# The opening of a fused retention and low-rank mixer kernel: its hand-written order written anew

## The chip, the cores and the metric

The kernel runs on one core of a Trainium2 chip. A core has a matrix engine (PE, with its weight loads listed apart as PEld), a vector engine (DVE), a scalar engine (ACT), a third elementwise engine (POOL) and a queue engine (SP) that here does nothing but issue transfers. Each engine takes its own instructions strictly in the order in which the program lists them; engines wait for one another through semaphores. The metric is device time in microseconds (us) of one execution.

## The reference

There are two parts. The first is a retention recurrence over a sequence of 768 steps, for 4 batches and 8 heads of width 64:

```
state = gamma[h] * state + outer(k[t], v[t])
y[t]  = scale * q[t] @ state
```

Its heads are laid side by side to x, 768 x 512 for each batch, and the second part is a mixer on x:

```
h   = xt @ U @ V                  # xt: x with rows and columns exchanged; rank 32
u   = x + h (turned back)
out = u + relu(u @ w_ch1) @ w_ch2 # 512 -> 2048 -> 512
```

## The kernel before

The recurrence is computed in 6 chunks of 128 steps. With decay factors put onto q and k beforehand, a chunk c needs: q and k scaled (`qd`, `kd`), turned by PE so that the head width lies on partitions (`turn_q`, `turn_k`) and copied out of PSUM (`evict_q`, `evict_k`); the scores of the chunk with itself (`scores`), masked by DVE (`keep`); v cast to bf16 (`cast_v`); the running sum of k times v (`sums`), copied to a bf16 state (`state`); and the output as the product of q with the state of the chunks before (`inter`) plus masked scores times v (`intra`), copied to x (`evict_x`). The state makes this a chain: `inter(c)` needs `state(c-1)`, and `sums(c)` may not write the running sum before `state(c-1)` has read it.

Then the mixer: `low` multiplies x by U, `evict_P` copies the result, `turn_x` and `high` build u with channels on partitions in PSUM, `evict_u` copies it, and the first large product (`mlp1`, with w_ch1) and the second (with w_ch2, by a scheme with fewer block products) follow. While the MLP of batch b runs, the recurrence of batch b+1 is woven into it at numbered slots.

Only batch 0 has nothing to be woven into. Its recurrence, from the start to the first `mlp1` matmul, is the opening, or ramp. Its order is written out by hand: one list of calls (lines 811 to 839 of the kernel before), each with its chunk or half and, where an engine can be chosen, the engine: G for POOL, V for DVE, A for ACT. The list sets the order on every engine at once. It also holds `run_idle(n, bank)`: n matmuls of zeros, 128 x 512, whose result nobody reads; another nine of them stand ahead of the list.

The inputs of batch 0 are asked for by SP ahead of the list in a fixed order: q0, kA, q1, k2, k3, vA, q2, k4, v2, k5, v3, v4, v5. (q0, q1, q2 hold two chunks each; kA and vA hold chunks 0 and 1. For the first two chunks of q, and likewise for the other pairs, even and odd steps are apart, so `turn_q(0, h)` needs both `qd(0, 0)` and `qd(0, 1)`.) Nothing in the list touches that queue. The slices of w_ch1 are asked for from POOL's queue (`load_w1`, line 161), those of w_ch2 too (line 167).

A helper records most operations, so many have one line number: PE work is L116 apart from the transposes L334 (k) and L346 (q); copies are L310 on ACT and L312 on DVE or POOL; L327 is `qd`, L322 `kd`, L368 `keep`. In the names, bk is a PSUM bank, st the state, a the masked scores, vb the cast v, qk the scaled q and k, q0T and kT the turned ones.

Of the kernel before, what the change touches and what calls it, by code (L numbers as in the profile page):

```python
# [47 lines left out]
def kernel(  # L48
# [17 lines left out]
    DH = moe_w_ch1.shape[1]  # L66
# [238 lines left out]
    G, V, A = nc.gpsimd, nc.vector, nc.scalar  # L305
# [503 lines left out]
        copy_by(eng, uTs[0][:, c, ts(hf, HS)], r0["u", hf, c])  # L809

    for f, *args in (
        (qd, 0, 0, V), (qd, 0, 1, G), (run_idle, 9, 5), (turn_q, 0, 1), (turn_q, 0, 0), (kd, 1, V),
        (evict_q, 0, 0, A), (run_idle, 4, 5), (turn_k, 1), (evict_k, 1, A), (kd, 0, G),
        (turn_k, 0), (evict_q, 0, 1, V), (run_idle, 1, 5), (scores, 1), (qd, 1, 1, V),
        (qd, 1, 0, G), (run_idle, 1, 2), (turn_q, 1, 0), (evict_k, 0, A), (scores, 0), (kd, 2, G),
        (keep, 1, 0), (kd, 3, G), (keep, 1, 1), (evict_q, 1, 0, A), (turn_q, 1, 1),
        (evict_q, 1, 1, A), (keep, 0, 1), (keep, 0, 0), (qd, 2, 1, G), (spread_V, 0),
        (spread_V, 1), (evict_V, 1, A), (turn_k, 2), (evict_k, 2, V), (run_idle, 2, 1),
        (turn_k, 3), (evict_k, 3, V), (evict_V, 0, A), (kd, 4, G), (scores, 2), (cast_v, 1, V),
        (kd, 5, G), (cast_v, 0, A), (run_idle, 2, 1), (sums, 0), (keep, 2, 0), (state, 0, A),  # L820
        (intra, 0), (keep, 2, 1), (scores, 3), (evict_x, 0, A), (sums, 1), (inter, 1), (intra, 1),
        (qd, 2, 0, V), (turn_q, 2, 1), (keep, 3, 0), (load_w1, 0, 256), (load_w1, DH // 2, 256),
        (turn_k, 4), (turn_q, 2, 0), (keep, 3, 1), (evict_x, 1, V), (evict_k, 4, V), (state, 1, A),
        (inter, 2), (evict_q, 2, 1, A), (cast_v, 2, V), (run_idle, 1, 0), (sums, 2),
        (evict_q, 2, 0, A), (scores, 4), (intra, 2), (state, 2, A), (inter, 3), (evict_x, 2, A),
        (turn_k, 5), (keep, 4, 1), (evict_k, 5, A), (turn_x, 0, 0), (cast_v, 3, V), (sums, 3),
        (keep, 4, 0), (intra, 3), (scores, 5), (turn_x, 0, 2), (state, 3, V), (cast_v, 4, A),
        (keep, 5, 1), (evict_x, 3, A), (sums, 4), (state, 4, A), (keep, 5, 0), (inter, 4),
        (intra, 4), (low, (0, 1, 2, 3)), (inter, 5, 1), (cast_v, 5, G, 1), (cast_v, 5, G, 0),
        (intra, 5, 1), (evict_x, 5, V, 1), (evict_x, 4, A), (inter, 5, 0), (intra, 5, 0),  # L830
        (turn_x, 0, 3), (turn_x, 0, 1), (low, (4,)), (evict_x, 5, A, 0), (low, (5,)),
        (evict_P, 0, A), (turn_x, 1, 1), (turn_x, 1, 2), (turn_x, 1, 0), (evict_P, 1, A),
        (high, 0, 0), (high, 0, 1), (evict_u, 0, 0, V), (evict_u, 0, 1, V), (high, 1, 0),
        (evict_u, 1, 0, A), (high, 0, 2), (turn_x, 1, 3), (high, 1, 2), (high, 0, 3),
        (evict_u, 0, 2, V), (evict_u, 0, 3, V), (high, 1, 1), (evict_u, 1, 1, V), (high, 1, 3),
        (evict_u, 1, 3, A), (evict_u, 1, 2, V), (load_w1, 256, 768),
        (load_w1, DH // 2 + 256, 256),
    ):
        f(*args)

# [124 lines left out]
```

## Time and profile before

| what | value |
|---|---|
| runs of the kernel before | 221.0, 221.14, 221.19 us (median 221.14) |
| the profiled execution | 222.94 us |
| its span, first to last instruction | 221.2 us |
| PE busy in the span | 213.1 us (96%) |
| mean granted TensorE clock | 0.992 |
| first `mlp1` matmul | 29.84 us from the span's start |
| idle matmuls | 29 in all, 20 of them in the list |

The times in the profile are us from the span's start. A row of the timeline gives start, duration, engine, line, operation, output <- inputs, shape and count, and in brackets how long the engine had been idle and who ended that. Rows that merge several instructions start with the first and end with the last. A matmul's end in these rows is some 0.16 us after the next one may start, so the next matmul's start and not the end says how long PE was taken, while a reader of the result waits for the end. The view by stretches gives for each the busy time of the engines and the granted clock (1.00 is full speed). The chain of waits goes back from the last instruction to what released it.

### The profile page before, as it was taken

How to read it: one execution, taken by the hardware profiler on the slowest of the kernel's cores; microseconds unless marked ns; L12 is line 12 of the kernel's file. 1: busy time of each engine (PE TensorE's matmuls, PEld its weight loads, DVE VectorE, ACT ScalarE, POOL GpSimd, SP SyncE). 2: the span in 40 equal slices, each digit the busy share in tenths (PEclk: the TensorE clock that was granted, in tenths of full speed). 3: DMA queues.
4: the chain of work that ended last, by engine and by line, in shares of the span. 5: the costliest groups of instructions: out<-in, count | busy, mean ns of one | idle time of the engine just before them, and what ended most of it. 6: DMA issues, size and time to landing. Idle time of an engine off the chain costs nothing.

```text
span 221.2 us, 5022 instructions
## 1 busy us (share of the span) xinstructions
PE 213.1 (96%) x1999; PEld 155.0 (70%) x1999; DVE 147.0 (66%) x295; ACT 119.7 (54%) x248; POOL 81.8 (37%) x91
## 2 busy tenths in 40 slices
PE   7898999999999999999999999998999999999993
PEld 2446665668888765667887876666887866668883
DVE  8577784798887873579974720889885601556662
ACT  3346847775148466778444737778434557771000
POOL 6656820003996401904233279550424430000000
PEclk9969999999999999999999999999999999999999
DMA  6999999999999968999999389998020570000222
GB/s 170 237 268 189 142 204 214 212 216 221 196 223 183 224 160 165 187 210 308 149 217 235 75 159 237 226 232 126 3 95 3 125 181 30 0 0 0 98 95 96
DMA packets 98583, 34.89 MB, mean 158 GB/s; under 512 B 86752, under 2 KB 94848, under 8 KB 98560
## 3 DMA queue, kind: packets, MB, share of 16 engines
q1 hardware_dynamic: 94112, 30.02, 67.9%
q0 software_dynamic: 4304, 4.29, 12.0%
q8 instruction: 15, 0.25, 0.5%
q10 hardware_dynamic: 144, 0.26, 0.3%
q14 instruction: 8, 0.07, 0.1%
HBM read 27.46 MB, written 6.29 MB: 153 GB/s over the span
## 4 chain that ended last, share of the span: by engine, by line
PE 89%; DMA 4%; ACT 2%; DVE 2%; POOL 1%; issue 1%; SPq 0%; ACTq 0%
PE bk L116 87%; DMA in<-in_q_dram 4%; PE bk L440 1%; ACT st L310 1%; POOL qk L327 1%; ACT P_sb L121 1%; PE bk L334 1%; DVE vb L312 1%; SPq L176 0%; DVE gs L621 0%; PE bk L346 0%; DVE state L508 0%; ACT x L480 0%; DVE x L312 0%; DVE kT L312 0%
## 5 line engine op out<-in xcount | busy, mean ns | idle before, releaser
L116 PE MATMUL bk<-uT,w1b 128*128 128x384 bf16 x512 | 85.7, 326 | 0.0
L116 PEld LDWEIGHTS <-w1b 128*128 128x128 bf16 x512 | 53.8, 106 | 29.6 <-issue 0.2
L121 ACT ACTIVATE gT<-bk 128x384 bf16<-128x384 f32 x125 | 61.1, 490 | 23.6 <-PE bk L116 23.4
L697 DVE TENSOR_TENSOR res<-bk,res 128x256 f32<-128x256 f32 (+2 forms) x66 | 30.3, 461 | 20.7 <-PE bk L116 19.6
L116 PEld LDWEIGHTS <-gT 128*128 128x128 bf16 x384 | 36.1, 98 | 7.6 <-issue 1.9
L116 PE MATMUL bk<-w2b,gT 128*128 128x256 bf16 x288 | 37.6, 273 | 0.0
L116 PEld LDWEIGHTS <-gs 128*128 128x128 bf16 x296 | 27.8, 98 | 4.5 <-DVE gs L621 0.9
L268 POOL TENSOR_TENSOR qk<-k_n,Gk 128x512 bf16<-128x512 f32 x18 | 19.9, 1105 | 25.0 <-DMA k_n<-in_k_dram 23.7
L621 DVE TENSOR_TENSOR gs<-gT 128x768 bf16<-128x768 bf16 (+1 forms) x20 | 10.5, 526 | 27.7 <-ACT gT L121 27.7
L116 PE MATMUL bk<-w2s,gs 128*128 128x256 bf16 x192 | 25.9, 273 | 0.6 <-DVE gs L621 0.6
L463 DVE TENSOR_TENSOR a<-bk,mask 128x512 bf16<-128x512 f32 x36 | 22.9, 681 | 1.6 <-PE bk L116 1.3
L562 DVE TENSOR_TENSOR res<-bk,x 128x512 f32<-128x512 f32 x24 | 15.9, 686 | 9.3 <-PE bk L116 9.2
L697 POOL TENSOR_TENSOR res<-s,res 128x512 f32<-128x512 f32 (+2 forms) x13 | 13.7, 1060 | 21.6 <-DVE res L697 16.2
L480 ACT ACTIVATE x<-bk 128x512 bf16<-128x512 f32 x18 | 10.7, 596 | 19.2 <-PE bk L116 16.9
L273 POOL TENSOR_TENSOR qk<-q_n,Gq 128x512 bf16<-128x512 f32 x18 | 19.7, 1097 | 0.3
L697 POOL TENSOR_TENSOR res<-c,res 128x256 f32<-128x256 f32 x12 | 8.7, 725 | 18.1 <-ACT c L692 18.0
L116 PE MATMUL bk<-w2s,gT 128*128 128x256 bf16 x96 | 13.4, 273 | 0.0
L279 ACT ACTIVATE vb<-v_n 128x512 bf16<-128x512 f32 x18 | 10.9, 624 | 4.1 <-DMA v_n<-in_v_dram 4.0
L116 PE MATMUL bk<-w2b,gs 128*128 128x256 bf16 (+1 forms) x104 | 13.1, 264 | 0.0
L621 DVE TENSOR_TENSOR gs<-gs,gT 128x768 bf16<-128x768 bf16 (+1 forms) x20 | 11.8, 591 | 0.7
L621 DVE TENSOR_TENSOR gT<-gT 128x768 bf16<-128x768 bf16 (+1 forms) x20 | 12.0, 598 | 0.0
L116 PE MATMUL bk<-idle 128*128 128x512 bf16 x29 | 10.5, 505 | 1.2 <-DVE idle L190 1.2
(99 smaller groups left out, 221.0 us busy)
## 6 DMA issues: line engine op xcount, KB each, us to landing
k_n<-in_k_dram SPq DMA_DIRECT2D x22, 256.0 KB, 5.1
v_n<-in_v_dram SPq DMA_DIRECT2D x22, 256.0 KB, 5.1
out_dram<-res SPq DMA_DIRECT2D x22, 256.0 KB, 2.8
q_n<-in_q_dram SPq DMA_DIRECT2D x18, 256.0 KB, 5.1
w2b<-in_moe_w_ch_dram POOLq DMA_DIRECT2D x4, 512.0 KB, 15.0
in<-in_q_dram SPq DMA_DIRECT2D x3, 512.0 KB, 6.3
w1b<-in_moe_w_ch_dram POOLq DMA_DIRECT2D x3, 256.0 KB, 5.3
w1b<-in_moe_w_ch_dram POOLq DMA_DIRECT2D x1, 768.0 KB, 7.9
```

The source lines that it names most:

```text
L116: nc.tensor.matmul(o, l, r, **kw)
L121: nc.scalar.activation(o, i, AF.Relu if relu else AF.Copy)
L268: eng.tensor_tensor(kd, k_n, Gk[:, c].unsqueeze(2).to_broadcast([P, H, D]), op=ALU.mult)
L273: eng.tensor_tensor(qd, rc[b, c]["q_n"], Gq[:, c].unsqueeze(2).to_broadcast([P, H, D]), op=ALU.mult)
L279: nc.scalar.activation(vb, rc[b, c]["v_n"], AF.Copy)
L310: nc.scalar.activation(o, i, AF.Copy)
L312: eng.tensor_copy(out=o, in_=i)
L463: nc.vector.tensor_tensor(r["a"][:, e], r["s"][e].rearrange("p (n t) -> p n t", n=NP), mask4, op=ALU.mult)
L480: nc.scalar.activation(x_of(b, c), o, AF.Copy)
L562: nc.vector.tensor_tensor(res_of(b, j), h, xs[b, j], op=ALU.add)
L621: nc.vector.tensor_tensor(o, x, y, op=op)
L697: eng.tensor_tensor(x, y, x, op=ALU.add)
```

## The change

The list of the opening is written anew. The same operations stand in it, for the same chunks and halves, in another order, and some go to another engine:

- from POOL to DVE: `kd(0)`, `kd(3)`; `qd(1, 0)` goes from POOL to DVE and `qd(1, 1)` from DVE to POOL; `qd(0, 0)` and `qd(0, 1)` trade places likewise.
- from DVE to ACT: `evict_k(2)`, `evict_k(3)`, `evict_x(1)`, `evict_q(0, 1)`, `evict_u(0, 0)`, `evict_u(0, 2)`, `evict_u(1, 2)`; from ACT to DVE: `evict_q(0, 0)`, `evict_k(1)`, `evict_x(4)`, half 1 of `evict_P`. `cast_v(0)` and `cast_v(1)` trade ACT and DVE.
- the idle matmuls in the list are 7, 9, 3, 1, 6, 2, 2 (30), before 9, 4, 1, 1, 2, 2, 1 (20). Eleven stand behind the turning of q1 (`turn_q(1, 0)`), before five.
- `load_w1` for the first two slices of 256 columns stands 16 and 13 entries earlier in the list, the other `load_w1` entries six.

Two lines of the list, which has 135 entries:

```diff
-        (qd, 0, 0, V), (qd, 0, 1, G), (run_idle, 9, 5), (turn_q, 0, 1), (turn_q, 0, 0), (kd, 1, V),
+        (qd, 0, 1, V), (qd, 0, 0, G), (run_idle, 7, 5), (turn_q, 0, 0), (qd, 1, 1, G), (kd, 1, V),
...
+        (evict_q, 1, 0, A), (evict_q, 1, 1, A), (turn_k, 2), (keep, 0, 1), (run_idle, 6, 1),
```

ACT's queue, from the eviction of q's second pair (`evict_q(1, 0)`, q0T) to that of x of chunk 0. Before:

```order
L310 ACTIVATE q0T_189<-bk1_12_264 128x2x2x128
L310 ACTIVATE q0T_189<-bk0_15_295 128x2x2x128
L310 ACTIVATE Vb_95<-bk7_17_307 128x384
L310 ACTIVATE Vb_95<-bk6_16_305 128x384
L310 ACTIVATE vb_0_0_344<-in0_97 128x512
L310 ACTIVATE st0_185<-bk7_24_349 64x4x64 x2
L310 ACTIVATE x_0_0_390<-bk6_25_361 128x512
```

and after:

```order
L310 ACTIVATE q0T_189<-bk1_11_269 128x2x2x128
L310 ACTIVATE q0T_189<-bk0_14_296 128x2x2x128
L310 ACTIVATE Vb_95<-bk6_16_304 128x384
L310 ACTIVATE kT_0_2_325<-bk3_18_311 128x512
L310 ACTIVATE Vb_95<-bk7_15_302 128x384
L310 ACTIVATE vb_0_1_346<-in0_97 128x512
L310 ACTIVATE st0_185<-bk7_22_350 64x4x64 x2
L310 ACTIVATE kT_0_3_390<-bk2_24_362 128x512
L310 ACTIVATE x_0_0_392<-bk6_25_370 128x512
```

The evictions of k of chunk 2 and of chunk 3 (kT_0_2, kT_0_3) have come in from DVE, the one ahead of the cast of v, the other between the state and x.

POOL's queue, from the scaling of q's second pair to the third slice of w_ch1. Before:

```order
L327 TENSOR_TENSOR qk_2_260<-in_97,Gq_168 128x512
L322 TENSOR_TENSOR qk_2_260<-k_n_2_101,Gk 128x512
L322 TENSOR_TENSOR qk_3_258<-k_n_3_103,Gk 128x512
L327 TENSOR_TENSOR qk_5_303<-in_97,Gq_168 128x512
L322 TENSOR_TENSOR qk_4_328<-k_n_4_107,Gk 128x512
L322 TENSOR_TENSOR qk_5_303<-k_n_5_111,Gk 128x512
L161 DMA w1b_428<-in_moe_w_ch_dram 128x4x256
L161 DMA w1b_430<-in_moe_w_ch_dram 128x4x256
L312 CAST vb_5_569<-v_n_5_117 128x256 x2
L161 DMA w1b_633<-in_moe_w_ch_dram 128x4x768
```

and after:

```order
L327 TENSOR_TENSOR qk_3_209<-in_97,Gq_168 128x512
L322 TENSOR_TENSOR qk_2_267<-k_n_2_101,Gk 128x512
L327 TENSOR_TENSOR qk_5_327<-in_97,Gq_168 128x512
L322 TENSOR_TENSOR qk_4_330<-k_n_4_107,Gk 128x512
L322 TENSOR_TENSOR qk_5_327<-k_n_5_111,Gk 128x512
L161 DMA w1b_348<-in_moe_w_ch_dram 128x4x256
L161 DMA w1b_367<-in_moe_w_ch_dram 128x4x256
L312 CAST vb_5_519<-v_n_5_117 128x256 x2
L161 DMA w1b_637<-in_moe_w_ch_dram 128x4x768
```

The scaling of k of chunk 3 has gone; the transfers of w_ch1 stand behind the same two instructions, the scalings of k4 and k5, as before.

DVE's queue, from the scaling of q's third pair to the cast of v of chunk 3. Before:

```order
L327 TENSOR_TENSOR qk_0_4_328<-in0_97,Gq0_168 128x512
L368 TENSOR_TENSOR a_0_3_381<-bk4_26_379,mask_174 128x512
L368 TENSOR_TENSOR a_0_3_381<-bk5_27_380,mask_174 128x512
L312 CAST x_0_1_443<-bk6_28_400 128x512
L312 COPY kT_0_4_445<-bk3_30_432 128x512
L312 CAST vb_0_2_455<-v_n_0_2_109 128x512
L368 TENSOR_TENSOR a_0_4_466<-bk5_35_465,mask_174 128x512
L312 CAST vb_0_3_504<-v_n_0_3_113 128x512
```

and after:

```order
L327 TENSOR_TENSOR qk_0_4_330<-in0_97,Gq0_168 128x512
L368 TENSOR_TENSOR a_0_3_404<-bk4_26_402,mask_174 128x512
L312 CAST vb_0_2_420<-v_n_0_2_109 128x512
L312 COPY kT_0_4_466<-bk3_30_445 128x512
L368 TENSOR_TENSOR a_0_3_404<-bk5_27_403,mask_174 128x512
L368 TENSOR_TENSOR a_0_4_476<-bk5_35_475,mask_174 128x512
L312 CAST vb_0_3_503<-v_n_0_3_113 128x512
```

x of chunk 1 has gone to ACT, and the cast of v of chunk 2 stands three instructions further forward, ahead of the eviction of k4 and of one of chunk 3's masks.

More of the change, by code (lines that the diff above doesn't have):

```diff
@@ L811 @@
     for f, *args in (
-        (qd, 0, 0, V), (qd, 0, 1, G), (run_idle, 9, 5), (turn_q, 0, 1), (turn_q, 0, 0), (kd, 1, V),
[L813 to L835, printed above, removed]
@@ L836 @@
-        (evict_u, 1, 3, A), (evict_u, 1, 2, V), (load_w1, 256, 768),
-        (load_w1, DH // 2 + 256, 256),
+        (qd, 0, 1, V), (qd, 0, 0, G), (run_idle, 7, 5), (turn_q, 0, 0), (qd, 1, 1, G), (kd, 1, V),
+        (kd, 0, V), (run_idle, 9, 5), (turn_q, 0, 1), (evict_q, 0, 0, V), (turn_k, 0), (turn_k, 1),
+        (evict_k, 1, V), (evict_q, 0, 1, A), (run_idle, 3, 5), (scores, 1), (evict_k, 0, A),
+        (qd, 1, 0, V), (turn_q, 1, 0), (scores, 0), (keep, 1, 1), (kd, 2, G), (keep, 1, 0),
+        (turn_q, 1, 1), (keep, 0, 0), (spread_V, 1), (spread_V, 0), (run_idle, 1, 2), (kd, 3, V),
@@ new lines @@
+        (evict_q, 1, 0, A), (evict_q, 1, 1, A), (turn_k, 2), (keep, 0, 1), (run_idle, 6, 1),
+        (evict_V, 0, A), (evict_k, 2, A), (qd, 2, 1, G), (evict_V, 1, A), (kd, 4, G), (kd, 5, G),
+        (scores, 2), (cast_v, 0, V), (cast_v, 1, A), (load_w1, 0, 256), (sums, 0), (run_idle, 2, 1),
+        (turn_k, 3), (load_w1, DH // 2, 256), (keep, 2, 1), (intra, 0), (keep, 2, 0), (state, 0, A),
+        (evict_k, 3, A), (evict_x, 0, A), (sums, 1), (scores, 3), (qd, 2, 0, V), (keep, 3, 0),
+        (inter, 1), (cast_v, 2, V), (state, 1, A), (intra, 1), (turn_q, 2, 1), (turn_k, 4),
@@ new lines @@
+        (evict_x, 1, A), (turn_q, 2, 0), (evict_q, 2, 1, A), (inter, 2), (run_idle, 2, 0),
+        (evict_k, 4, V), (keep, 3, 1), (sums, 2), (evict_q, 2, 0, A), (scores, 4), (intra, 2),
+        (keep, 4, 1), (state, 2, A), (turn_k, 5), (evict_x, 2, A), (cast_v, 3, V), (inter, 3),
+        (sums, 3), (evict_k, 5, A), (cast_v, 4, A), (keep, 4, 0), (cast_v, 5, G, 1), (intra, 3),
+        (turn_x, 0, 1), (state, 3, V), (scores, 5), (turn_x, 0, 0), (turn_x, 0, 2), (sums, 4),
+        (evict_x, 3, A), (keep, 5, 0), (state, 4, A), (inter, 4), (intra, 4), (keep, 5, 1),
@@ new lines @@
+        (low, (0, 1, 2, 3)), (inter, 5, 0), (inter, 5, 1), (cast_v, 5, G, 0), (evict_x, 4, V),
+        (intra, 5, 1), (intra, 5, 0), (turn_x, 0, 3), (evict_x, 5, V, 1), (evict_x, 5, A, 0),
+        (low, (4,)), (low, (5,)), (turn_x, 1, 2), (evict_P, 0, A), (turn_x, 1, 0), (high, 0, 0),
+        (evict_P, 1, V), (high, 0, 1), (evict_u, 0, 0, A), (evict_u, 0, 1, V), (high, 1, 0),
+        (high, 0, 3), (turn_x, 1, 1), (high, 0, 2), (high, 1, 1), (evict_u, 0, 3, V), (turn_x, 1, 3),
+        (high, 1, 3), (load_w1, 256, 768), (load_w1, DH // 2 + 256, 256), (high, 1, 2),
@@ L838 @@
+        (evict_u, 0, 2, A), (evict_u, 1, 3, A), (evict_u, 1, 0, A), (evict_u, 1, 1, V),
+        (evict_u, 1, 2, A),
     ):
```

## The prediction

> **What bounds the kernel now.** I read the chain of waits first.
>
> ```profile
> PE 89%; DMA 4%; ACT 2%; DVE 2%; POOL 1%; issue 1%; SPq 0%; ACTq 0%
> ```
>
> PE sets the end for 89% of the span, and the change touches only the opening. In order of time the chain there reads (start, duration, what):
>
> ```profile
> 1.88 7.95 DMA in<-in_q_dram
> ...
> 17.03 0.38 ACT st L310
> ...
> 20.49 1.12 DVE vb L312
> ...
> 21.66 0.40 PE bk L116 x4
> ...
> 22.14 0.39 ACT st L310
> ...
> 25.36 0.39 ACT st L310
> ...
> 26.82 30.74 PE bk L116 x214
> ```
>
> Its first long piece is a transfer: q1 lands at 1.88 + 7.95 = 9.83, POOL scales it, PE turns it. The timeline of PE shows that, and a shorter wait ahead of it:
>
> ```profile
> 9.78 0.42 PE L116 MATMUL bk<-q0T,kT 64*64 64x128 bf16 x16 [0.25 <-ACT kT L310]
> ...
> 11.50 0.40 PE L346 MATMUL bk<-ident,qk 128*128 128x128 bf16 x4 [0.98 <-POOL qk L327]
> ```
>
> No edit reaches SP's queue, so q1's landing stays. From 26.82 it is PE without a break, so whatever the opening gains at its end the whole kernel gains. The question is the stretch between. The view by stretches (us; busy us of PE, PEld, DVE, ACT, POOL; granted clock; DMA), cut at the length that the clock shows, 3.41 us:
>
> ```profile
> 9.32:12.73 3.41, 2.19 (x45) 1.17 (x43) 2.30 (x4) 1.70 (x4) 2.83 (x3) 1.00 1.21 250
> 12.73:16.14 3.41, 3.41 (x22) 1.55 (x20) 2.45 (x6) 1.91 (x4) 0.94 (x2) 0.50 1.28 266
> ...
> 19.56:22.97 3.41, 2.46 (x38) 1.61 (x36) 2.58 (x4) 2.12 (x5) 2.54 (x3) 1.00 0.76 166
> ```
>
> In the stretch to 12.73 PE was busy 2.19 of 3.41 us, 64%, and for exactly the next 3.41 us the granted clock is 0.50. In the stretch to 22.97 it was busy 72% and kept the clock. So in this execution the point at which PE loses its clock lies between 64% and 72%, and the half clock costs PE up to 3.41 x 0.5 = 1.71 us, in the middle of the opening.
>
> The second loss is a meeting of DVE and POOL. In the timeline of POOL stand:
>
> ```profile
> 9.90 1.55 POOL L327 TENSOR_TENSOR qk<-in,Gq 128x512 bf16<-128x512 f32 x1 [1.21 <-DMA in<-in_q_dram]
> 15.91 1.04 POOL L327 TENSOR_TENSOR qk<-in,Gq 128x512 bf16<-128x512 f32 x1 [2.47 <-DMA in<-in_q_dram]
> 20.28 1.04 POOL L322 TENSOR_TENSOR qk<-k_n,Gk 128x512 bf16<-128x512 f32 x1 [1.82 <-DMA k_n<-in_k_dram]
> 21.26 1.56 POOL L161 DMA_DIRECT2D w1b<-in_moe_w_ch_dram  x2
> ```
>
> and in that of DVE:
>
> ```profile
> 9.85 0.69 DVE L327 TENSOR_TENSOR qk<-in,Gq 128x512 bf16<-128x512 f32 x1 [1.29 <-DMA in<-in_q_dram]
> 12.32 1.29 DVE L368 TENSOR_TENSOR a<-bk,mask 128x512 bf16<-128x512 f32 x2 [0.58 <-PE bk L116]
> 20.41 1.19 DVE L312 CAST vb<-v_n 128x512 bf16<-128x512 f32 x1
> 23.04 0.42 DVE L312 CAST vb<-v_n 128x512 bf16<-128x512 f32 x1
> ```
>
> The one that comes second waits: DVE started `qd` at 9.85, and POOL's took 1.55 in place of 1.04; POOL started `kd(5)` at 20.28, and DVE's cast of v2 ended only at 21.60 instead of taking 0.42. PE stood for that cast until 21.66.
>
> **The change, part by part.** The sum is made against the profiled execution (222.94 us, span 221.2) by walking the new queues from 11.5 on. The durations are these rows of ACT:
>
> ```profile
> 9.13 1.08 ACT L310 ACTIVATE kT<-bk 128x512 bf16<-128x512 bf16 x2 [0.34 <-PE bk L334]
> 11.93 1.42 ACT L310 ACTIVATE q0T<-bk 128x512 bf16<-128x512 bf16 x2 [1.72 <-PE bk L346]
> 13.21 0.86 ACT L310 ACTIVATE Vb<-bk 128x384 bf16<-128x384 f32 x2
> 14.01 0.63 ACT L310 ACTIVATE vb<-in 128x512 bf16<-128x512 f32 x1
> 17.83 0.60 ACT L310 ACTIVATE x<-bk 128x512 bf16<-128x512 f32 x1
> 18.50 0.77 ACT L310 ACTIVATE st<-bk 64x256 bf16<-64x256 f32 x2
> 19.80 1.33 ACT L310 ACTIVATE q0T<-bk 128x512 bf16<-128x512 bf16 x2 [0.54 <-PE bk L346]
> ```
>
> and of PE:
>
> ```profile
> 16.31 0.62 PE L116 MATMUL bk<-vb,qk 64*128 64x128 bf16 x8
> 18.48 0.38 PE L116 MATMUL bk<-st,q0T 128*128 128x128 bf16 x4
> 19.37 0.40 PE L346 MATMUL bk<-ident,qk 128*128 128x128 bf16 x4
> 21.97 0.40 PE L116 MATMUL bk<-q0T,kT 64*128 64x128 bf16 x8
> 27.24 0.42 PE L116 MATMUL bk<-x,Ub 128*32 128x512 bf16 x2
> 28.14 0.82 PE L116 MATMUL bk<-Vb,P_sb 128*128 128x384 bf16 x4
> 29.62 0.38 PE L116 MATMUL bk<-P_sb,Vb 128*128 128x512 bf16 x1
> 29.84 3.41 PE L116 MATMUL bk<-uT,w1b 128*128 128x384 bf16 x20
> ```
>
> 1. *Up to 11.5: nothing.* POOL's `qd(1, 1)` now comes first, 9.90 to 10.94, and DVE's `qd(1, 0)`, which is queued behind an eviction, waits for it and ends near 11.5 (after its wait the cast above needed some 0.3 us more, a `qd` takes 0.69 in all, so 0.3 to 0.69). PE turns q1 at 11.55, 0.05 later. Idle matmuls and turnings ahead of that fill time that PE has.
>
> 2. *The clock.* With three idle matmuls and both k turnings moved behind 9.3, PE has one wait between `scores(1)` and 11.55, about 0.7 us, so it is busy (3.41 - 0.7) / 3.41 = 79% of that stretch: above 72%. I take the full clock throughout.
>
> 3. *To the first state.* ACT is now the bound: from 11.97 the two q0T (1.42), both Vb (0.86), k2 (0.54, half of the pair) and the cast of v1 (0.63) stand in a row: 11.97 + 3.45 = 15.42. The six idle matmuls (0.22 each, as the last PE rows' 512-column matmul from 29.62 to 29.84) end near 14.6 and are hidden behind that. The second half of `sums(0)` ends at 15.42 + 0.43 = 15.85 (four matmuls to their end, 0.40, and the handing over), before at 16.31 + 0.62 = 16.93. The state can start 1.1 us sooner.
>
> 4. *A part is given back.* ACT then does state (0.77), k3 (0.54, new here) and x0 (0.60): 15.88 + 1.91 = 17.79, so `inter(1)` runs at 17.83, before 18.48: 0.65 left of the 1.1. From there to `turn_q(2, 1)` PE needs 19.37 - 18.48 = 0.89 as before: 18.72.
>
> 5. *The cast of v2.* It now stands ahead of k4's eviction. v2 was asked for at 11.97:
>
> ```profile
> v_n<-in_v_dram SPq DMA_DIRECT2D x1, 256.0 KB, 7.1
> ```
>
> So it lands at 19.07, DVE (free from 18.3) casts it to 19.5, ahead of POOL's 20.28: no meeting. What is late next is ACT: x1 (new here, from 18.83, 0.60), then q2's two evictions (1.33): 20.76. The two idle matmuls wait in bank 0 for the first of them, near 20.1, and take 0.43, so `sums(2)` runs at 20.56 (before 21.66, 1.10 sooner) and `scores(4)` at 20.80 (before 21.97).
>
> 6. *To the last state.* State 2 at 21.0 in place of 22.14. Then ACT: state, x2, k5 (0.77 + 0.60 + 0.54) to 22.9. k5 is no bound (`kd(5)` ends at 21.32). Then v4's cast (0.63):
>
> ```profile
> 17.66 2.23 SPq L136 DMA_DIRECT2D v_n<-in_v_dram  x2
> v_n<-in_v_dram SPq DMA_DIRECT2D x2, 256.0 KB, 4.7
> ```
>
> v4, first of the pair, lands near 17.66 + 4.7 = 22.4, in time. The cast ends at 23.55; PE is free by then, `sums(4)` runs at 23.8 and the last state at 24.2, before 25.36: 1.16 sooner. From there to `low(5)` the same matmuls follow (1.04 us from 26.20 to 27.24), so 26.08.
>
> 7. *The tail.* The two halves of P go to ACT and DVE side by side, but half 0 alone decides, so `high` starts 0.82 us after `low(5)` in place of 0.90 (28.14 - 27.24). Behind that stand two turnings in place of one (0.17 more). Net 0.09 lost: `mlp1` at 29.84 - 1.16 + 0.09 = 28.77.
>
> 8. *w_ch1 "sooner": nothing.* On POOL's queue the transfers stay behind `kd(4)` and `kd(5)`, and for k5 POOL waits until 20.28; they start at 21.3 as before. They do not bind:
>
> ```profile
> w1b<-in_moe_w_ch_dram POOLq DMA_DIRECT2D x1, 256.0 KB, 3.7
> ```
>
> The first slice lands at 21.26 + 3.7 = 25.0, ahead of 28.77; PE waits 0 for it. If it were late, `mlp1` would be late by as much.
>
> The sum is 29.84 - 28.77 = **1.07 us**. The profiled execution would go from 222.94 to 221.87. The runs shown have a median of 221.14, 1.80 below the profiled one; taking the same 1.07 from them gives **220.05 us**.
>
> *What the trace does not show* is DVE's cast of v3 (now at about 21.9) while POOL issues the two transfers (21.26 to 22.82); no whole cast stood beside such an issue before. Bounds: nothing, or the cast waits until 22.82, some 0.9 us, which goes through `sums(3)` to the last state and leaves about 0.2 us of gain. I take nothing, by the nearest row: the cast of v2 ended at 21.60 although POOL had been issuing since 21.26. Both ends stay in the range. [...] Above, the gain can be at most about the 1.71 us of half clock, as ACT's row of evictions already fills the time from 12 on: 219.4.
>
> **The rivals.**
>
> *The half clock is not in the timed runs: slower.* Then the kernel before has its 1.7 us already. At full clock its first `sums` waits only for its two casts (ACT from 14.01 to 14.64, DVE, free at 12.32 + 1.29 = 13.61, two evictions of k and its cast, three times about 0.4, to 14.8) and runs at 14.84, not 16.31; its chain is ahead by 1.4 us, so its cast of v2 falls before POOL's 20.28 too; it meets v2 (19.07), k5 and v4 a little earlier than the new one does, which carries k2, k3 and x1 on ACT (0.54 + 0.54 + 0.60 = 1.7 us more in that engine's row). I walk it to `mlp1` at about 28.15, so the change costs 28.77 - 28.15 = 0.6 us: **221.75 us**. [...] For it: the profiled execution is 1.80 us above the median, nearly that price. Against it: the three runs agree within 0.19 us, which a loss that comes and goes would not let them. [...]
>
> *The new order loses its clock too: no change.* If PE's busy share before 12.73 stays under the 64 to 72%, seven idle matmuls behind 13.1 cost 0.43 each, so `scores(2)` slips from 14.75 to 16.3 and the rest by 1.3: 28.77 + 1.3 = 30.07, **221.4 us**. For it: nothing but that the point is known only between two values. Against it: 79%.
>
> *The cast of v3 waits for POOL:* gain 0.2, **220.9 us**.
>
> **How the numbers follow.** The forecast 0.50, by itself 219.4 to 220.9; half clock absent 0.25; clock lost in both 0.10; cast of v3 0.12; other 0.03. About 0.2% (0.44 us) is what a measurement here can tell from no change. Of the forecast's half 0.46 lies beyond 0.44 us of gain, with 0.04 from the others: faster 0.50. Same: 0.04 of it, 0.05, 0.06 and 0.10 of the others: 0.25. Slower 0.25, nearly all from the absent half clock. The range runs from 219.4 to 221.75, the middle of that rival, so about half of it and a little at the low end are left out.
>
> **What would show it.** In the new profile: granted clock 1.00 from 12 to 20 (step 2); first state near 15.9, `inter(1)` near 17.8 (3, 4); a cast of v2 of 0.42 us that starts near 19.1 (5); last state near 24.2, `mlp1` at 28.8 (6, 7); first transfer of w_ch1 at 21.3 (8). Wrong would be a cast of v3 near 1.2 us, a clock of 0.50 anywhere in it, or a time that does not move although `mlp1` starts a microsecond sooner: then the timed runs before had no half clock.

## The result and the profile after

The changed kernel is slower, not faster: 222.22 us (median of 10 runs, 221.74 to 223.61) against 221.09 (10 runs, 220.98 to 221.23), a ratio of 1.0059 with a 95% interval of 1.0042 to 1.0075. That is 1.13 us, with 220.05 forecast; the time lies above the range too (219.4 to 221.75).

The changed kernel's profiled execution took 223.61 us, its span 220.4. Its opening ends almost where it was walked to end. Its view by stretches (columns as before):

```profile
9.32:12.73 3.41, 2.99 (x55) 1.66 (x53) 2.93 (x6) 2.21 (x4) 2.32 (x2) 1.00 1.28 248
12.73:16.14 3.41, 3.25 (x35) 1.95 (x36) 2.93 (x6) 2.75 (x7) 0.49 (x1) 1.00 1.28 267
```

The clock is 1.00, and PE is busy 88% of the first stretch. Its chain of waits, in order of time:

```profile
11.28 0.40 PE bk L346 x4
...
15.51 0.38 ACT st L310
15.91 0.38 ACT st L310
16.31 0.60 ACT kT L310
16.91 0.50 ACT x L310
17.45 0.97 PE bk L116 x20
18.44 0.60 ACT x L310
19.03 0.64 ACT q0T L310
...
20.90 0.69 DVE a L368
21.59 0.64 DVE vb L312
22.28 1.79 PE bk L116 x33
24.10 0.39 ACT st L310
24.50 0.39 ACT st L310
24.93 1.91 PE bk L116 x23
26.87 29.58 PE bk L116 x200
```

First state at 15.51, last at 24.10, and its timeline of PE has the first `mlp1` matmul at 28.73:

```profile
28.73 1.46 PE L116 MATMUL bk<-uT,w1b 128*128 128x384 bf16 x8
```

So the profile of the kernel before has `mlp1` at 29.84 and that of the changed one at 28.73, 1.11 us sooner, and yet the runs are 1.13 us slower. The span tells where the contradiction sits. The profiled execution of before had a span of 221.2 us; of 138 timed executions of the same kernel, run for the experiments, none showed a mean clock under 0.997 and the median span is 219.3. The changed kernel's ten spans are 220.0 to 220.5. The profile of before was the odd one.

### The profile page after: what moved, and what is told of

It is laid out like the page before. It is cut to its first block, busy times and chain, and to the rows that moved or that the text cites. A ratio compares the mean times of both kernels' runs of the same rounds, so it can differ in the third digit from the quotient of the medians.

```text
span 220.4 us, 5037 instructions
## 1 busy us (share of the span) xinstructions
PE 212.7 (97%) x2006; PEld 155.1 (70%) x2009; DVE 146.4 (66%) x294; ACT 120.5 (55%) x251; POOL 78.6 (36%) x89
## 4 chain that ended last, share of the span: by engine, by line
PE 90%; ACT 3%; DMA 2%; DVE 2%; issue 1%; POOL 1%; ACTq 0%; POOLq 0%
PE bk L116 88%; DMA in<-in_q_dram 2%; PE bk L440 1%; POOL qk L327 1%; ACT st L310 1%; PE bk L346 1%; ACT P_sb L121 1%; ACT x L310 0%; DVE gs L621 0%; DVE qk L327 0%; PE bk L334 0%; DVE a L368 0%; DVE vb L312 0%; ACT q0T L310 0%; DVE state L508 0%
## 5 line engine op out<-in xcount | busy, mean ns | idle before, releaser
L567 ACT ACTIVATE x<-res 128x512 bf16<-128x512 f32 x15 | 9.1, 628 | 4.5 <-DVE res L562 4.5
```

Of the source, the lines that this page charges most:

```text
L567: nc.scalar.activation(xs[b, j], res_of(b, j), AF.Copy)
```

## The experiments

Unless told otherwise, times are medians, and each ratio is against runs of the kernel before on the same chip in the same session (221.03 to 221.15). Three marks are followed: the first `mlp1` matmul (what the opening takes), from there to the span's end, and the time around the span (a run's time less its span). PE turns q1 at 11.50 in the first profile of the kernel before and between 10.99 and 11.28 in those of the changed kernel and of experiments 1 to 7, though no edit reaches q1's transfer. So an `mlp1` read from one profile is good to some 0.3 us, and the spans of the timed executions are the surer measure.

**1. The kernel before once more, no edit.**

> The kernel before, unchanged, to see span and clock of its timed executions. Theory 1 (the half clock of the profiled execution is not in the timed runs; 221.1 less the 1.74 us around the span is a span of 219.4): executions with a span near 219.4 and a mean clock of 1.00 are the rule, and one with 221.2 and 0.992 the exception; a profile without the half clock starts mlp1 near 28.0 in place of 29.84. Theory 2 (the half clock is in every execution, and the change loses its time outside the opening or outside the span): spans near 221.2 and clock 0.992 throughout, mlp1 at 29.8.

Measured: 221.09 us, ratio 1.0004 (0.9996 to 1.0013); twelve spans of 219.1 to 219.7. This profile is a usual one. Its stretches:

```profile
9.32:12.73 3.41, 2.48 (x48) 1.26 (x46) 2.59 (x5) 1.69 (x3) 3.13 (x3) 1.00 1.27 249
12.73:16.14 3.41, 3.37 (x53) 2.16 (x53) 3.33 (x7) 2.43 (x7) 0.94 (x2) 1.00 1.28 267
```

its chain of waits:

```profile
13.40 6.87 DMA k_n<-in_k_dram
...
20.34 1.05 POOL qk L322
...
21.44 0.40 PE bk L334 x4
...
23.64 0.39 ACT st L310
24.04 0.39 ACT st L310
24.47 0.62 PE bk L116 x12
25.09 30.74 PE bk L116 x214
```

and its `mlp1`:

```profile
28.11 2.11 PE L116 MATMUL bk<-uT,w1b 128*128 128x384 bf16 x12
```

PE's turning of q1 and its first `sums` are

```profile
11.20 0.40 PE L346 MATMUL bk<-ident,qk 128*128 128x128 bf16 x4 [0.93 <-POOL qk L327]
14.57 0.62 PE L116 MATMUL bk<-vb,qk 64*128 64x128 bf16 x8
```

and stand at 11.50 and 16.31 in the first profile. So of the 1.73 us between the two `mlp1` 0.30 came ahead of the half clock, with q1; behind the turning the first `sums` came after 4.81 us there and after 3.37 here, 1.44 apart.

At full clock the opening of the old order takes 28.11 us, 0.62 less than the new one's 28.73, and what its chain waits for is k5, whose transfer lands at 20.27. The half clock that the change was to remove is not there to be removed.

**2. The kernel before, PE's wait ahead of q1 filled.**

```diff
-        (qd, 1, 0, G), (run_idle, 1, 2), (turn_q, 1, 0),
+        (qd, 1, 0, G), (run_idle, 5, 2), (turn_q, 1, 0),
```

> The kernel before with five idle matmuls in place of one ahead of the turning of q1, where PE stood for 0.98 us in the profile (four of 0.216 us are 0.86). PE is then busy about 90% of the stretch before 12.73, so the clock should stay whole. Theory 1: timed runs the same, 221.1 within 0.2; the profiled span falls to about 219.4. Theory 2: timed runs about 1.5 us faster, 219.6.

Measured: 221.13, ratio 1.0006 (0.9997 to 1.0015), `mlp1` at 28.03. Work that keeps PE busy through that wait (3.26 of 3.41 us in the stretch from 9.32) brings nothing, as there is no loss of clock to prevent.

**3. The kernel before with six idle matmuls fewer**, between the turnings of q0 and q1.

```diff
-(evict_q, 0, 0, A), (run_idle, 4, 5), (turn_k, 1)
+(evict_q, 0, 0, A), (turn_k, 1)
-(evict_q, 0, 1, V), (run_idle, 1, 5), (scores, 1)
+(evict_q, 0, 1, V), (scores, 1)
-(qd, 1, 0, G), (run_idle, 1, 2), (turn_q, 1, 0)
+(qd, 1, 0, G), (turn_q, 1, 0)
```

> The kernel before with the six idle matmuls taken out that stand between the turning of q0 and that of q1 (20 in the list become 14), to let PE's busy share fall ahead of 12.7. If the half clock follows a stretch of 3.41 us under 64 to 72% busy, most executions now show a mean clock of 0.992 and a span of 221 us; the time is 1.5 us longer, 222.6. If the opening is bound by transfers whatever PE's clock is: spans of 219.5, 221.1.

Measured: 221.63 (221.21 to 224.83), ratio 1.0021 (0.9998 to 1.0045). Now the half clock is in timed runs, in some of them. Of twelve executions five have a mean clock of 0.998 to 1.000 and spans of 219.4 to 219.5; three have 0.992 (one half-clock stretch: 3.41 x 0.5 us is 0.008 of the span) and 219.9; three 0.985 and 221.2 to 221.8; one 0.969 and 223.1. The profile is one of those with 0.992; its stretches have

```profile
12.53:15.94 3.41, 3.19 (x22) 1.62 (x23) 2.56 (x7) 1.66 (x4) 0.94 (x2) 0.50 1.26 266
```

again 3.41 us long (in the same view 9.32:12.73 has 0.97 and 12.73:16.14 has 0.53). So the loss is real, and it comes and goes between executions; with the six idle matmuls in place it is in none of the 138 timed executions of the kernel before. By the first `sums` it had cost the same in both profiles that have it: that comes 4.75 us behind the turning of q1 here (11.05 to 15.80), 4.81 in the first profile of before, 3.37 without it. Behind that the two part. Here DVE's cast of v2 ran from 19.96 in 0.42 us, and 0.50 us are left at `mlp1` (28.61 against 28.11); in the first profile the cast met POOL's scaling of k5 (1.19 us from 20.41), and all of it was left. One program, then, has the half clock in only some executions: 7 of these 12 have a mean clock of 0.992 or less. Its place is known from one profile each of two programs (12.73 and 12.53), which does not settle whether it moves.

**4. Of the change only ACT's part**, in the kernel before.

```diff
-(evict_k, 2, V)
+(evict_k, 2, A)
...
-(evict_k, 3, V)
+(evict_k, 3, A)
...
-(evict_x, 1, V)
+(evict_x, 1, A)
```

> Of the change only this: in the kernel before, the evictions of k2, k3 and of x of chunk 1 go from DVE to ACT. Theory (the new order costs 0.62 us because ACT's row carries 0.54 + 0.54 + 0.60 us more): mlp1 from 28.11 to 28.5 to 28.8, ACT has 251 instructions, so the 0.32 us wait at 129 is there too, total 221.7 to 222.1. Rival (the idle matmuls or the exchanges of DVE and POOL carry it): mlp1 near 28.1, and only the wait at 129 adds 0.2 to 0.3: 221.1 to 221.4.

Measured: 222.04, ratio 1.0050 (1.0035 to 1.0064): nearly the whole loss of the change. Its timeline of ACT:

```profile
13.07 1.10 ACT L310 ACTIVATE kT<-bk 128x512 bf16<-128x512 bf16 x2
14.03 0.53 ACT L310 ACTIVATE Vb<-bk 128x384 bf16<-128x384 f32 x1
14.40 0.67 ACT L310 ACTIVATE vb<-in 128x512 bf16<-128x512 f32 x1
...
18.26 0.60 ACT L310 ACTIVATE x<-bk 128x512 bf16<-128x512 f32 x1 [1.04 <-PE bk L116]
18.76 0.76 ACT L310 ACTIVATE st<-bk 64x256 bf16<-64x256 f32 x2
```

and of PE:

```profile
15.12 0.60 PE L116 MATMUL bk<-vb,qk 64*128 64x128 bf16 x8 [0.44 <-ACT vb L310]
...
28.73 1.46 PE L116 MATMUL bk<-uT,w1b 128*128 128x384 bf16 x8
```

The first `sums` stands for ACT's cast and starts at 15.12 (14.57 in the usual profile of before, where DVE makes those evictions), and `mlp1` is at 28.73, 0.62 later: the theory's number. So these three evictions are enough, in the old order, to cost what the whole change costs in the opening. The kernel has 251 ACT instructions, and the wait of experiment 9 stands in it too (at 129.43), so some 0.2 us of its total are not the opening's.

**5. Of the change only the idle matmuls behind q1**, in the kernel before.

```diff
-(evict_k, 2, V), (run_idle, 2, 1)
+(evict_k, 2, V), (run_idle, 7, 1)
...
-(cast_v, 2, V), (run_idle, 1, 0)
+(cast_v, 2, V), (run_idle, 2, 0)
```

> Of the change only the idle matmuls behind the turning of q1: in the kernel before, two become seven ahead of the turning of k3, and one becomes two ahead of sums of chunk 2. The five stand in front of the turning of k3 and of scores of chunk 2, 0.22 us each, in a row where PE waits for ACT. Theory (idle matmuls are not the cost): mlp1 moves by 0 to 0.3, 221.1 to 221.4. Rival (they stand in front of scores of chunk 2 and so of the first state): mlp1 later by 0.6 to 1.1, 221.7 to 222.2.

Measured: 221.49, ratio 1.0021 (1.0013 to 1.0030), `mlp1` at 28.51. Between the two forecasts: 0.40 us. With ACT's row short, the seven are what the first `sums` waits for (they run from 12.89, and it starts at 15.59). 0.62 and 0.40 together would be 1.02, and the change has 0.62. That in the new order the idle matmuls lie in the time for which ACT's row makes PE wait anyway would explain it, and is not shown by itself.

**6. The changed kernel, k2 and k3 back on DVE.**

```diff
-(evict_k, 2, A)
+(evict_k, 2, V)
...
-(evict_k, 3, A)
+(evict_k, 3, V)
```

> The changed kernel with the evictions of k2 and k3 back on DVE. Theory A (the changed order is slow since ACT's row of evictions sets the pace, two evictions of 0.54 us of it new ahead of x0): x0 starts about 0.5 us sooner (16.3 in place of 16.8), inter(1) near 16.95 in place of 17.45, mlp1 0.3 to 0.5 sooner than 28.73; runs near 221.8. Theory B (the idle matmuls set the pace): mlp1 within 0.1 us of 28.73, runs 222.2.

Measured: 221.92, ratio 1.0043 (1.0030 to 1.0056), `mlp1` at 28.55. Only 0.18 of the 0.62 came back, and that is less than q1 alone came sooner in this profile (turned at 10.99 against 11.28); the median span fell by 0.15, to 220.05. In its profile ACT stands 0.49 us ahead of x of chunk 0, waiting for PE: the idle matmuls and the turning of k3 stand ahead of `intra(0)`.

**7. The changed kernel, eleven idle matmuls behind q1 cut to three.**

```diff
-(run_idle, 1, 2)
...
-(run_idle, 6, 1)
+(run_idle, 3, 1)
...
-(run_idle, 2, 1)
...
-(run_idle, 2, 0)
```

> The changed kernel with three idle matmuls in place of eleven behind the turning of q1 (of 1, 6, 2, 2 the 6 become 3, the others go). Theory A: the ACT row stays, mlp1 at 28.5 to 28.7, runs within 0.2 of 222.2. Theory B: the two idle matmuls behind the first sums (0.43 us) and the two that wait in bank 0 for q2's eviction are on the path: mlp1 0.4 to 0.9 us sooner, runs near 221.5. If the waits opened by it cost the clock, the granted clock shows 0.50 in a stretch of 3.41 us and the runs are over 222.5.

Measured: 221.84, ratio 1.0038 (1.0023 to 1.0053), `mlp1` at 28.99 in its profile, which is that of the longest of its six executions (span 220.5 against a median of 220.05; v2 landed only at 19.26 in it).

**8. Both edits together** (6 and 7).

> The changed kernel with both edits that helped a little each: k2 and k3 evicted on DVE again, and three idle matmuls in place of eleven behind the turning of q1. If ACT's row and the idle matmuls each hold the other's gain back (x0 waits for k3 on ACT or, without it, for the matmuls behind two idle ones), together they give more than the two alone (0.3 and 0.4 us): mlp1 near 28.2, runs 221.2 to 221.4. If they only add up: 221.5. If the transfers' landing (v2 at 19.1, k5 at 20.3) is what is left: no better than 221.7.

Measured: 222.09, ratio 1.0039 (1.0023 to 1.0056), `mlp1` at 29.01. No better than either. In its profile DVE is the row that decides: its `qd(1, 0)`, started at 10.63, took 1.51 us beside POOL (0.80 to 0.98 in the profiles of the changed kernel and of experiments 6 and 7), and four masks, the scaling of k3 (which the change also gave to DVE) and an eviction stand behind it, so `scores(2)` runs at 15.53. None of these edits brings the old opening back. It fits that the change filled DVE, ACT and PE at once, but that is argued from the profiles, not shown.

**9. The kernel before with ACT's instruction count of the changed one:** three copies of 128x1 among the constants, 251 ACT instructions in place of 248.

```diff
+    scr = consts.tile([P, 4], fp32)
+    for n in range(3):
+        nc.scalar.activation(scr[:, n : n + 1], lsc, AF.Copy)
```

> The kernel before with three tiny ACT copies (128x1) in ACT's free time near 4.5 us, so that ACT has 251 instructions, as in the changed kernel, in place of 248. In the profile of the changed kernel ACT stands 0.32 us without a releaser near 129.4 us and holds PE up; that of the kernel before has no such piece. Theory F (the wait belongs to the instruction's place in ACT's stream): the same piece of 0.3 us shows near 128.8 and the runs are 0.3 us slower, 221.35. Theory G (it comes from the new order's state, or is chance): no such piece, 221.05.

Why this was tried: from `mlp1` to the end the changed kernel takes 220.4 - 28.73 = 191.67 us, the usual profile of before 219.5 - 28.11 = 191.39, though the work there is the same. The chain of waits of the changed kernel has, in the MLP of a later batch,

```profile
124.90 4.49 PE bk L116 x41
...
129.43 0.32 issue
129.75 0.39 ACT c L692
```

where that of the kernel before, in its usual profile, is one piece of PE:

```profile
124.94 10.20 PE bk L116 x74
```

ACT waits 0.32 us for nothing that the profile shows, and PE for ACT. Measured: the wait is there (at 129.09), as forecast. But the total was 220.48, ratio 0.9965 (0.9951 to 0.9980): *faster* than the kernel before, and neither theory had that. Its profile does not show the gain: it is that of its longest execution (221.39), with `mlp1` at 28.04.

**10. The same once more.**

> The kernel before with three copies of 128x1 on ACT among its constants, as once already (220.48, ratio 0.9965), for a second profile. If the gain belongs to the program: 220.3 to 220.7, ratio 0.995 to 0.998, span near 218.7, and this profile shows where the 0.7 us went. If it belonged to the chip or the hour: 221.0 to 221.3. In both cases the wait of ACT of 0.32 us ahead of the copy to c at 129 is there, as in every kernel of 251 ACT instructions.

Measured: 220.39, ratio 0.9970 (0.9959 to 0.9981), `mlp1` at 27.20, the wait there again. The gain belongs to the program. In the view of transfers, cut to the first 30 us, q takes 5.0 us in it and 6.3 in the kernel before: the little tile has moved every tile allocated behind it by 32 bytes. The compiled program tells the rest: the targets of the input transfers started 224 bytes above a multiple of 256 in each partition (that of q at byte 202464), and now start at one (202496).

**11. The changed kernel with the same three copies.**

> The changed kernel with the same three copies of 128x1 on ACT. If what they do belongs to any order (the 0.67 us gained in the kernel before): 221.5. If it hangs on the instruction count of ACT, now 254: the 0.32 us wait of ACT ahead of the copy to c falls elsewhere in its stream, 221.7 to 222.2, and the span from mlp1 to the end is 191.3 to 191.4 in place of 191.67. If neither: 222.2 and 191.67 as before.

Measured: 222.20, ratio 1.0049 (1.0032 to 1.0066). Its transfers are as fast (q 5.3 us), the wait at 129 is gone (254 instructions), and it gains nothing: `mlp1` is at 29.25. POOL's scalings start earlier with the transfers, and the cast of v of chunk 0 on DVE, at 14.32, met one and took 1.09 us, so the first `sums` starts at 15.47. The old order was waiting for transfers; the new one waits for its own rows.

**12. The place alone: 32 bytes, no copies.**

```diff
-    lsc = consts.tile([P, 1], fp32)
+    lsc_w = consts.tile([P, 16], fp32)
+    lsc = lsc_w[:, 0:1]
```

> The kernel before, with one small constant widened from 4 to 64 bytes in a partition, so that every tile allocated behind it lies 32 bytes further on: the targets of the input transfers start at a multiple of 256 bytes in place of 224 above one. No copies on ACT, 248 ACT instructions. Theory (the gain of the three copies came from where their little tile moved the others): q's transfers take 5.0 us in place of 6.3, mlp1 at 27.2, no wait of ACT at 129, 219.9 to 220.3. Rival (the copies on ACT themselves do it): 6.3 us, mlp1 28.1, 221.0 to 221.2.

**13. 96 bytes** (the same edit with 32 columns).

> The same with 96 bytes: the targets start at 64 above a multiple of 256 bytes, that is at a multiple of 64 but not of 256. If a multiple of 64 is enough: as with 32 bytes, q in 5.0 us, 219.9 to 220.3. If it must be a multiple of 256: q in 5.5 to 6.3 us, 220.6 to 221.2.

Measured: with 32 bytes 220.57, ratio 0.9974 (0.9964 to 0.9985), `mlp1` at 27.25; with 96 bytes 220.81, ratio 0.9989 (0.9978 to 1.0001), `mlp1` at 27.69. The view of transfers for the first 30 us, SP's queue (packets, MB, share of 16 engines' time) and the transfers of q; 32 bytes:

```profile
q1 hardware_dynamic: 13520, 4.72, 61.8%
...
in<-in_q_dram SPq DMA_DIRECT2D x3, 512.0 KB, 5.0
```

96 bytes:

```profile
q1 hardware_dynamic: 13520, 4.72, 72.6%
...
in<-in_q_dram SPq DMA_DIRECT2D x3, 512.0 KB, 6.3
```

and the kernel before, unmoved:

```profile
q1 hardware_dynamic: 13520, 4.72, 72.5%
...
in<-in_q_dram SPq DMA_DIRECT2D x3, 512.0 KB, 6.3
```

The same packets take 15% less time (61.8 against 72.5%) where the targets start at a multiple of 256 bytes, and no less where they start 64 above one (that of q at 202560). The gain comes with the place of the targets, not with the copies. That 96 bytes may still have gained a little (its interval ends at 1.0001) is not explained by the transfers.

**14. The wait at 129 by itself:** the kernel before with the three copies, their tile 256 bytes wide (`scr = consts.tile([P, 64], fp32)`), so that alignment is as before.

> The kernel before with the three copies on ACT again, their little tile made 256 bytes wide, so that every target lies at 224 above a multiple of 256 as before; 251 ACT instructions. This measures the wait of ACT at 129 by itself. Theory: q in 6.3 us, mlp1 28.0 to 28.1, the wait of 0.32 us is there, mlp1 to the end 191.6 to 191.7 in place of 191.4, 221.3 to 221.5. Rival (the copies bring the gain): mlp1 near 27.2, 220.4.

Measured: 221.28, ratio 1.0011 (1.0002 to 1.0019), `mlp1` at 27.94, from there to the end 219.5 - 27.94 = 191.56. The transfers of q take 6.3 us again. The wait costs about 0.2 us. It stands in all six profiles of kernels with 251 ACT instructions (five programs) and in none with 248, 249 or 254.

**15. The changed kernel with the same** (254 ACT instructions, alignment as it was).

> The changed kernel with the same three copies and the same tile of 256 bytes: 254 ACT instructions, targets where they were. Theory (the second part of the loss hangs on the count of ACT's instructions): no wait of 0.32 us at 130, mlp1 28.7, mlp1 to the end 191.3 to 191.4 in place of 191.67, 221.8 to 222.0. Rival (it belongs to the new order in some other way): 222.2 with 191.6 or more.

Measured: no wait at 129, `mlp1` to the end 219.7 - 28.36 = 191.34 as forecast, but the total 222.20, ratio 1.0048 (1.0031 to 1.0065), as without the edit. Its six spans have a median of 220.05 (220.2 in the changed kernel), while the time around the span was up to 2.82 us.

**16. The kernel before with ten more matmuls** (128 columns each, in PE's wait ahead of q1), as many as the changed kernel has.

```diff
-(run_idle, 1, 2), (turn_q, 1, 0)
+(run_idle, 1, 2), (run_idle, 10, 2, 128), (turn_q, 1, 0)
```

> The kernel before with ten idle matmuls of 128 columns more (about 0.6 us) in PE's wait of 0.93 us ahead of the turning of q1, so that PE has as many instructions as in the changed kernel. There the time around the span was 1.74 to 3.2 us (median 1.8), in the kernel before 1.72 to 1.83. Theory P (the longer PE stream costs time outside the span in some executions): span 219.3 as before, time around it up to 2.0 or more in some runs, median 0.05 to 0.2 higher. Otherwise both as before, 221.05.

Measured: 221.25, ratio 1.0011 (0.9993 to 1.0029), `mlp1` at 27.86. The opening is not longer in the profile, but three of the twelve executions have a mean clock of 0.990 to 0.992 and spans of 220.3 to 220.7. That is the mean clock that one half-clock stretch leaves (0.992 in the first profile of before), and it comes with more work for PE ahead of q1 here, not with less. Experiments 8 and 17 have one such execution each. None of these was profiled, so where the clock was lost in them is open. The time around the span is 1.72 to 1.95 us, above 1.84 in five of twelve executions. Over all of this section's kernels with ten more matmuls, the changed one included, it is above 1.84 in 16 of 40 executions (up to 3.21); over all others here in 0 of 146. Six more (experiment 5) did not bring it out. The traces hold a lead: in the profiled executions of the changed kernel (3.21 us around the span) and of experiment 15 (2.82) a transfer of 0.02 MB in a queue that the view calls instruction starts some 2 us behind the last instruction, at 222.6 and 221.6. No other profile has one there, those of experiments 6, 11 and 16 with ten more matmuls included (1.79 to 2.05 around the span). That it is what lengthens these executions was not tested.

**17. The changed kernel with eight idle matmuls fewer and 254 ACT instructions** (the edits of 7 and 15 together).

> The changed kernel without eight of its eleven idle matmuls behind the turning of q1 (the program of 221.84, PE 2001 instructions), and with the three copies on ACT and the tile of 256 bytes, so 254 ACT instructions. Theory (three separate losses: 0.62 in the opening, 0.2 by the wait of ACT at 129, 0.2 to 0.3 around the span from ten more matmuls): only the first is left: time around the span 1.72 to 1.84 in every execution, no wait at 129, mlp1 to the end 191.3 to 191.4, 221.6 to 221.8. Rival (the losses do not add, and the last 0.2 is something else of the order): 221.85 or more.

Measured: 221.87 (220.73 to 223.29), ratio 1.0037 (1.0016 to 1.0057). All three marks came as the theory has them: around the span 1.73 to 1.83, no wait at 129, `mlp1` at 28.63 and 220.0 - 28.63 = 191.37 from there. The total lies 0.07 above the theory's band and just in the rival's: with one time in ten near 220.7 and one near 223.3 (mean clock 0.990) it does not tell the two apart.

**18. The kernel before, moved by 32 bytes, with one idea of the change:** the cast of v2 ahead of x of chunk 1 and of k4's eviction.

```diff
-(keep, 3, 1), (evict_x, 1, V), (evict_k, 4, V)
+(keep, 3, 1), (cast_v, 2, V), (evict_x, 1, V), (evict_k, 4, V)
...
-(evict_q, 2, 1, A), (cast_v, 2, V),
+(evict_q, 2, 1, A),
```

> The kernel before with its tiles moved by 32 bytes (220.57) and one idea of the change, its step 5: the cast of v2 on DVE stands ahead of the evictions of x of chunk 1 and of k4. With the early transfers that cast ran from 17.87 to 19.02, beside POOL's scaling of k5 at 17.70, and PE stood for it until 19.07. Theory: it now runs at 16.7 to 17.1, the sums of chunk 2 at 18.2 to 18.4, mlp1 at 26.6 to 27.0 in place of 27.25, 219.9 to 220.3. Rival (the eviction of k4, now later, meets POOL in its place, or v3's landing binds the next step): mlp1 27.1 to 27.4, 220.4 to 220.7.

Measured: 220.03 (219.53 to 220.79), ratio 0.9961 (0.9948 to 0.9974): faster than both kernels, and the fastest here. DVE's cast in the kernel moved by 32 bytes alone:

```profile
17.87 1.15 DVE L313 CAST vb<-v_n 128x512 bf16<-128x512 f32 x1
```

and with the cast put first:

```profile
17.45 0.41 DVE L313 CAST vb<-v_n 128x512 bf16<-128x512 f32 x1
```

So the idea of step 5 is sound where that meeting happens. Its own profile is one of its longer executions (span 218.7 against a median of 218.3) with `mlp1` at 27.16, so the 26.6 to 27.0 of the theory was not seen. In it DVE's scaling of q's third pair met POOL (1.53 us in place of 0.68 in the profile of experiment 12), which put the cast later than the theory's 16.7 to 17.1. How much of the 0.54 us against experiment 12 is the cast's is not shown.

## Why the prediction was wrong

By its own steps, all measured in the changed kernel's profile:

1. *Up to 11.5, nothing:* q1 is turned at 11.28, in the usual profile of before at 11.20. Right.
2. *The clock:* 79% and full clock were forecast; it was 88% and full clock. Right for the changed kernel.
3. *First state* 15.88 forecast, 15.51 measured.
4. *`inter(1)`* 17.83, measured 17.45; k3's eviction stands ahead of x0, as the step said.
5. *Cast of v2* at 19.1 in 0.42, measured at 19.02 in 0.43, without a meeting; `sums(2)` 20.56, measured 20.15.
6. *Last state* 24.2, measured 24.10.
7. *`mlp1`* 28.77, measured 28.73.
8. *w_ch1, nothing:* its transfers start at 21.18 (21.26 before). Right.

The cast of v3 beside POOL's issue, for which there was no row, took 0.71 in the changed kernel and 0.43 in the usual profile of before. POOL's and DVE's timelines of the changed kernel:

```profile
21.18 1.56 POOL L161 DMA_DIRECT2D w1b<-in_moe_w_ch_dram  x2
```

```profile
21.51 0.71 DVE L312 CAST vb<-v_n 128x512 bf16<-128x512 f32 x1
```

So it costs at most 0.3, near the end that was taken.

The mechanism of these steps was right, but that the end came out to 0.04 us is luck. Up to `sums(2)` the changed kernel was about 0.4 sooner than walked, 0.27 of it because q1 was turned at 11.28 and not at 11.55; from `sums(2)` to the last state it took 0.31 longer, with the cast of v3 on the chain. Counted from the turning of q1, the first profile of before needs 18.34 us to `mlp1` and the changed kernel 17.45: 0.89 gained, where the walk has 1.12.

**The step that failed is the last one: "taking the same 1.07 from them".** The walk of 1.07 us came within 0.04 of the two profiles' difference in `mlp1`, 1.11. But the profiled execution of before, which took 222.94 us, held a stretch of half clock, and the runs to which the difference was carried over did not. The number that said so stood in the prediction: the profile was 1.80 us above the median. And 222.94 - 221.2 = 1.74 us lay around its span, as much as around the spans of the runs (1.72 to 1.84), so the 1.80 was inside the span. It was put in the rival's favour, and then outweighed by "the three runs agree within 0.19 us, which a loss that comes and goes would not let them". That argument counts against a loss that is in some of the runs; it says nothing against one that is in none of them. The sign that the prediction itself gave for this came: `mlp1` a microsecond sooner in the profile, and the time no better. (The subtraction is off by 0.02 besides: 221.14 - 1.07 is 220.07.) The prediction also carried a gain in the opening to the whole kernel in full; the changed kernel takes 0.28 us longer behind `mlp1`, a term for which the prediction had nothing.

The rival held at 0.25, "the half clock is not in the timed runs", was the mechanism, and its walk was good: `mlp1` of before at 28.15, measured 28.11; first `sums` 14.84, measured 14.57; a cost of 0.6, measured 0.62. (Here too q1 was turned 0.30 sooner than walked, and the rest took 0.26 longer; the two walks are short by nearly the same, so their difference holds.) The reason that it gave, k2, k3 and x1 in ACT's row, is shown by experiment 4 to be enough by itself in the old order. In the new order it is not the only hold: with k2 and k3 back on DVE (experiment 6) the opening stayed long.

What was missing in it is the rest: 221.75 forecast, 222.22 measured. By the timed runs, the spans differ by 220.2 - 219.3 = 0.9 us, and the medians of the totals by 0.2 more: (222.22 - 220.2) - (221.09 - 219.3). That 0.2 is not in every execution: the time around the span has a median of 1.80 in the changed kernel and of 1.77 in the 138 of the kernel before, but in four of the ten executions it is 2.00 to 3.21. Within the span, 0.62 is the opening and 191.67 - 191.39 = 0.28 comes behind it; the wait of 0.32 us of ACT accounts for it, and experiment 14 prices it at about 0.2 in the kernel before. The long times around the span go with the ten more matmuls: experiment 16 brings them out by the matmuls alone, though only up to 1.95, and they are absent wherever eight of the ten are taken out. In the changed kernel itself these parts did not come off one by one in the median (15 and 17), so their sizes there, about 0.1 to 0.2 us, stay open. Why ACT stands there, and how more matmuls lengthen what is around the span, was not shown.

## What to carry to other kernels

Before a difference is walked in a profile, compare the profiled execution's span with the spans of the timed runs: where they differ by more than the runs among themselves, the profile shows something that the runs do not have, and a gain that removes it is no gain. A loss that is in only some executions is to be weighed by how often it occurs, and an order that pays for its removal on every execution (k2, k3 and x1 on ACT, six idle matmuls more behind the turning of q1) must win that back from a few. Where the opening waits for transfers, look at where their targets start before the order is changed: 32 bytes gained about 0.5 us here, and the new order lost 1.1.

## What was not expected of the hardware

- Targets that start at a multiple of 256 bytes in a partition (that of q at 202496) came with input transfers 15% shorter in engine time (61.8 against 72.5%) and q's 5.0 us in place of 6.3; a place 64 above such a multiple did not (202560: 72.6%, 6.3 us), nor did two places 224 above one (202464: 72.5%, 6.3 us; 202720, experiment 14: 73.0%, 6.3 us). Why was not shown, nor that it has to be a multiple of 256: of these four places 202496 is also the only multiple of 128.
- Three instructions more on ACT (251 in place of 248), whether copies among the constants or evictions in the opening, put a wait of 0.32 us into its stream some 100 us later, at 128.4 to 129.7; with six more it was gone again.
- Ten more matmuls of 128 columns made the time around the span longer in 5 of 12 executions, by up to 0.1 us; ten more of 512, in the changed kernel, in 4 of 10, by up to 1.4.
- A mean clock of 0.992 or less came with six idle matmuls fewer in 7 of 12 executions, in none of 138 timed ones with all of them, and again in 3 of 12 with ten more. PE's busy share was 72% in a stretch behind which the clock stayed whole (19.56 to 22.97 in the first profile of before), 64% in the stretch ahead of the half clock there, and 57% (1.96 of 3.41 us from 9.32 to 12.73) in experiment 3, where the half clock begins at 12.53; these shares alone do not say in which executions it is lost.
